# Attention and two feed-forward layers on one core: a plain second slot, and later low parts of W_out

## The chip, the cores and the metric

The kernel runs on one core of one Trainium2 chip. The metric is the device time of one execution in microseconds (us). The kernel before takes 766.02 us (median of 3 runs, 765.67 to 766.97).

## The reference

Attention over 2 batches, 8 heads, 768 positions and 64 elements a head, in which a query sees only the keys whose nearest of 16 centroids is its own, then two feed-forward layers on 1536 tokens (512 to 2048 to 512 elements):

```python
mask = q_assign[:, :, :, None] == k_assign[:, :, None, :]
scores = np.where(mask, scale * np.matmul(q, k.transpose(0, 1, 3, 2)), -1e9)
attn = np.exp(scores - np.max(scores, axis=-1, keepdims=True))
x = np.matmul(attn / (np.sum(attn, axis=-1, keepdims=True) + 1e-09), v)
...
h = x @ w_in;  x = (h * (1.0 / (1.0 + np.exp(-1.702 * h)))) @ w_out
h = x @ w_in2; r = np.maximum(h, 0.0); out = (r * r) @ w_out2
```

The four weight matrices come as 64-bit floats. The kernel reads their bits and makes 32-bit floats of them on the chip.

## The kernel before, in words

**Precision.** TensorE multiplies with operands of the type fp32r. A matrix is split in a high part (ACT's cast) and a low part (what is left, by DVE), and a product of two matrices is three products: high by high, high by low, low by high.

**Order.** The attention takes up the first third. The feed-forward layers follow in 32 slots, `q` = 0 to 31: two layers, two batches of 768 tokens, and `NP` = 8 slots of 256 hidden elements each. The first pass is slots 0 to 7, layer 0 for batch 0. Every engine works through its own queue in the order in which the program issues the instructions; this order is written out by hand in the loop over `slots` (from L1084 on), and the tile framework puts in the waits. SP's queue holds nearly all DMAs.

**A slot** makes two chunks of 128 hidden elements (`ga` and `gb`) for 768 tokens, in four blocks of 128 by 384 in two banks of PSUM, A and B_. The plain form (`hidden`, L143) needs four block products of 12 matmuls each. The other form (`product`, L1006) is Strassen's scheme in Winograd's order: seven products of 6 matmuls, from sums of blocks of x (S1 to S4, `folds`, L160) and of W_in (T1 to T4, `Weights.sums`, L976). For it ACT copies three products from PSUM to SBUF and DVE adds three others to them (`total`, L860; DVE's rows with L864). `active` (L868) is the gelu, twice on ACT (L876 the high part, L877 in full), and `low` (L879) the low part on DVE (L880). Slot 0 is plain, slots 1 to 31 are Strassen's.

**The parts of W_in.** `Weights` holds the two chunks of a slot in `wb` and their block sums in `wt`. `sums` is four DVE operations (L979 to L982). `early(0)`, `early(1)` and `late` split them in high and low parts (`part`: ACT L985, DVE L986). The first two products need `early(0)`, the next two `early(1)`, the last three `late`.

**W_out's work.** `second` (L882) multiplies the gelu's result by W_out; a slot leaves it to the next one, which does it in four quarters of 12 matmuls, `before(0)` to `before(3)`, between its own products. In slots 2 to 7 the first two quarters take chunk `gb`, the other two `ga`.

**Decoding.** Every 128 rows or columns of a weight matrix are one task (`tasks`, L1020), in an order fixed ahead: W_in and W_out of the first pass by turns. A task goes through these steps: `fetch` (L1027), a DMA of 512 KB on SP into one of three raw buffers; `absolute` (L1033), the magnitude on ACT (L98 and L100); `step(0)` and `step(1)`, the decoding on DVE (L112 and L115); and `step(2)`, which writes a W_in task to DRAM (`keep`, L136; its DMA is L138) or splits a W_out task (`parts`, L119: ACT's cast L121, DVE's low part L122), and asks for the fetch of the task three further on. `COUNTS` (L1013) says how many tasks a slot does: 2 in slot 0, 4 each in slots 1 to 6, 1 in slot 7. All W_out tasks of the first pass use one tile, `room`, so the magnitude of one waits until the one before it has been split. W_in tasks go into `wb`.

**The order in slots 1 to 7** (from L1138 on): A gets the product B11 with A11, ACT copies it to `h`; B_ gets B21 with A12; first task; `total(0, LO)`; quarter 0; second task; products T2 and T1 (A and B_ again, after ACT's copy and after the total); sums and `early` of the next slot; quarter 1; products T3 and B22; the third task with its split; `total(1, HI)` and `total(1, LO)`; the gelu of `gb`; the fourth task; quarter 2; product T4, which needs A back from `total(1, HI)`; quarter 3. In slots 3 to 6 there is one more DVE operation (`nxt.sum`, L946), in slot 7 five splittings of batch 1's x (`nxt.part`).

**The way from the attention to slot 1.** In the last 14 tiles of the attention GpSimd splits the four quarters of batch 0's x (L792, L793) and folds them to S1 to S4 (L796), beside the merges of the heads' results (L588) and the normalisation (L616). Behind the loop DVE decodes chunk 2 of W_in (`mags[4]`), SP fetches the raw data of chunk 3 into the buffer that this sets free and then the norms' rows (`spread`), and DVE does the last merge. Chunk 2 is copied by a DMA into `weights[1]` (L1072) and split (`early(0)`, L1073). In slot 0 chunk 3 is decoded; then come the sums and `early(1)` for slot 1, the magnitude and decoding of chunk 4, and the splitting of S1 to S4 (`fold`, L955) between them.

## Time and profile before

| | |
|---|---|
| time, median of 3 runs | 766.02 us (765.67 to 766.97) |
| the profiled execution's own time | 766.92 us |
| its span, first to last instruction | 765.1 us |
| granted TensorE clock, mean over the span | 0.995 |
| busy: PE, DVE, ACT, GpSimd | 97%, 76%, 74%, 22% |
| the first pass of the feed-forward layers | about 244 to 378 us |

In the rows, times are us from the first instruction; L12 is line 12 of the kernel. PE is TensorE's matmuls (PEld its weight loads, which overlap them), DVE is VectorE, ACT ScalarE, POOL GpSimd and SP the queue that issues DMAs. In a timeline a row gives the start, the time it took, the engine, the line, what it writes and reads with its shape, and how many like it were merged to one row. In square brackets stand the idle time of the engine before it and what ended that. One instruction overlaps the next of its engine a little, so that the distance between two starts is shorter than the time of the first. A granted clock of 1.00 is 2.4 GHz, one of 0.50 is 1.2 GHz.

### The profile page before, as it was taken

How to read it: one execution, taken by the hardware profiler on the slowest of the kernel's cores; microseconds unless marked ns; L12 is line 12 of the kernel's file. 1: busy time of each engine (PE TensorE's matmuls, PEld its weight loads, DVE VectorE, ACT ScalarE, POOL GpSimd, SP SyncE). 2: the span in 40 equal slices, each digit the busy share in tenths (PEclk: the TensorE clock that was granted, in tenths of full speed). 3: DMA queues.
4: the chain of work that ended last, by engine and by line, in shares of the span. 5: the costliest groups of instructions: out<-in, count | busy, mean ns of one | idle time of the engine just before them, and what ended most of it. 6: DMA issues, size and time to landing. Idle time of an engine off the chain costs nothing.

```text
span 765.1 us, 12063 instructions
## 1 busy us (share of the span) xinstructions
PE 744.8 (97%) x4303; PEld 680.0 (89%) x4303; DVE 579.0 (76%) x1011; ACT 568.0 (74%) x1138; POOL 169.3 (22%) x226
## 2 busy tenths in 40 slices
PE   8999999999999599999999999999999999999998
PEld 5999999999999588888899999998899898988996
DVE  7988998988997888888776777777776787553441
ACT  7999999999898777787686666767767676553441
POOL 5848667667675000000000000000000000000000
PEclk9999999999999899999999999999999999999999
DMA  8886676794222545445154233313443203101002
GB/s 211 176 205 141 137 195 196 157 210 98 68 52 59 173 164 174 156 160 180 56 169 162 99 122 110 119 61 97 153 149 111 83 29 112 54 28 56 0 1 83
DMA packets 72235, 91.15 MB, mean 119 GB/s; under 512 B 30384, under 2 KB 54096, under 8 KB 72080
## 3 DMA queue, kind: packets, MB, share of 16 engines
q1 hardware_dynamic: 71632, 90.26, 41.1%
q8 instruction: 34, 0.56, 0.3%
q14 instruction: 25, 0.20, 0.1%
q10 hardware_dynamic: 544, 0.13, 0.1%
HBM read 61.12 MB, written 13.94 MB: 98 GB/s over the span
## 4 chain that ended last, share of the span: by engine, by line
PE 79%; DVE 10%; ACT 8%; issue 1%; DMA 0%; POOL 0%; DVEq 0%; ACTq 0%; SPq 0%; POOLq 0%
PE ps L1010 23%; PE y L899 17%; PE pa L565 8%; PE pt L540 8%; PE y L893 6%; PE ps L516 4%; PE ps L518 4%; PE y L895 3%; ACT gh L876 2%; ACT h L877 2%; PE ps L369 1%; DVE h L864 1%; DVE rr L112 1%; ACT oh L121 1%; PE pt L306 1%
## 5 line engine op out<-in xcount | busy, mean ns | idle before, releaser
L553 DVE TENSOR_TENSOR el<-pt,eh 128x384 fp32r<-128x384 f32 x192 | 97.6, 550 | 11.1 <-ACT eh L550 10.4
L522 DVE TENSOR_REDUCE nm<-ps 128x1 f32<-128x768 f32 x96 | 91.5, 954 | 11.6 <-PE ps L518 10.0
L876 ACT ACTIVATE gh<-h 128x384 fp32r<-128x384 f32 (+1 forms) x72 | 47.8, 664 | 60.6 <-DVE h L866 32.3
L531 ACT ACTIVATE e<-ps,nm 128x768 f32<-128x768 f32 x96 | 87.7, 913 | 2.8 <-DVE nm L522 2.3
L550 ACT CAST eh<-pt 128x384 fp32r<-128x384 f32 x192 | 83.2, 489 | 5.7 <-PE pt L540 4.0
L880 DVE TENSOR_TENSOR gl<-h,gh 128x384 fp32r<-128x384 f32 (+1 forms) x97 | 65.7, 681 | 22.2 <-ACT h L877 14.3
L540 PE MATMUL pt<-identF,e 128*128 128x128 f32 x576 | 80.2, 274 | 0.8 <-DVE el L553 0.6
L899 PE MATMUL y<-oh,gl 128*128 128x512 f32 x192 | 75.2, 391 | 0.0
L899 PE MATMUL y<-ol,gh 128*128 128x512 f32 x192 | 75.0, 390 | 0.0
L899 PE MATMUL y<-oh,gh 128*128 128x512 f32 x192 | 74.9, 390 | 0.0
L1010 PE MATMUL ps<-xh,wxh 128*128 128x384 f32 x248 | 64.9, 343 | 8.6 <-ACT h L1144 7.8
L516 PE MATMUL ps<-k,q 128*128 128x512 f32 x192 | 68.9, 361 | 1.0 <-ACT e L531 1.0
L540 PEld LDWEIGHTS pt<-identF,e 128*128 128x128 f32 x576 | 65.3, 140 | 3.2 <-DVE el L553 2.4
L1010 PE MATMUL ps<-xl,wxh 128*128 128x384 f32 x248 | 64.2, 340 | 0.0
L1010 PE MATMUL ps<-xh,wxl 128*128 128x384 f32 x248 | 63.9, 339 | 0.0
L518 PE MATMUL ps<-k,q 80*128 80x512 f32 x192 | 60.9, 340 | 0.0
L1010 PEld LDWEIGHTS ps<-xh,wxh 128*128 128x128 f32 x248 | 43.3, 190 | 12.9 <-ACT h L1144 8.1
L1010 PE MATMUL ps<-xh,wyh 128*128 128x384 f32 x186 | 48.0, 339 | 4.9 <-DVE h L864 4.9
L893 PE MATMUL y<-gl,oh 128*128 128x512 f32 x128 | 50.2, 392 | 0.0
L893 PE MATMUL y<-gh,ol 128*128 128x512 f32 x128 | 50.1, 392 | 0.0
L893 PE MATMUL y<-gh,oh 128*128 128x512 f32 x128 | 50.1, 392 | 0.0
L877 ACT ACTIVATE h<-h 128x384 f32<-128x384 f32 (+1 forms) x72 | 47.8, 665 | 2.3
(223 smaller groups left out, 1884.5 us busy)
## 6 DMA issues: line engine op xcount, KB each, us to landing
raw<-in_moe_w_in_dram SPq DMA_DIRECT2D x32, 512.0 KB, 4.1
raw<-in_moe_w_out_dram SPq DMA_DIRECT2D x32, 512.0 KB, 4.2
wb<-wst SPq DMA_DIRECT2D x24, 512.0 KB, 4.3
q<-k SPq DMA_DIRECT2D x15, 384.0 KB, 5.8
wst<-room SPq DMA_DIRECT2D x16, 256.0 KB, 2.4
wst<-wb SPq DMA_DIRECT2D x13, 256.0 KB, 2.5
k<-k SPq DMA_DIRECT2D x16, 192.0 KB, 5.1
rawv<-in_v_dram SPq DMA_DIRECT2D x8, 384.0 KB, 4.9
```

What stands on the lines that cost most here:

```text
L516: nc.tensor.matmul(ps[:, a:a + n], q2[:, qs], k2[:, a:a + n], start=True, stop=False)
L518: nc.tensor.matmul(ps[:, a:a + n], q1[0:K1, qs], k1[0:K1, a:a + n], start=False, stop=True)
L522: nc.vector.tensor_reduce(out=nm, in_=live["s", t][:, 0:S], op=ALU.max, axis=AX, negate=True)
L531: nc.scalar.activation(e, live["s", t][:, 0:S], ACTF.Exp, bias=live.pop(("nm", t)), accum_out=sums[:, s:s + 1])
L540: nc.tensor.transpose(pt[:, i], e[:, kc * P:(kc + 1) * P], identF)
L550: nc.scalar.copy(place("eh", t, u), live["pt", t, u])
L553: nc.vector.tensor_tensor(out=place("el", t, u), in0=live.pop(("pt", t, u)), in1=f32(place("eh", t, u)), op=ALU.subtract)
L876: nc.scalar.activation(g[0][:, at], src, of)
L880: nc.vector.tensor_sub(g[1][:, at], h[:, c, at], f32(g[0][:, at]))
L893: nc.tensor.matmul(y[m], l[:, cs], r[:, 0:512], start=first, stop=last)
L899: nc.tensor.matmul(y[m], l[:, m * P:(m + 1) * P], r, start=(begin and z == 0), stop=(fc == KF - 1 and z == 2))
L1010: nc.tensor.matmul(ps, w[a][:, wi, kc * P:(kc + 1) * P], x[z][kc], start=start and j == kc == 0, stop=j == 2 and kc == 1, skip_group_check ...
```

## The change

- **Slot 1 becomes plain.** It takes a branch of its own: four times `hidden`, with the parts of the two W_in chunks as they are (`Weights.plain` splits them into the tile that held B11, B21, T1 and T2, `sides` are its two halves), the gelu straight from PSUM, no sums, no late parts, no copies and no totals. The DMA that copied chunk 2 into `weights[1]` is gone. The order of its tasks and quarters is written anew: quarters 0 and 1 behind the second block product, 2 and 3 behind the fourth.
- **The splitting of S1 to S4** moves from slot 0 to slot 1. Slot 0 keeps the plain split of chunk 3, the decoding of chunk 4 and now the magnitude of the next task too.
- **Slots 2 to 7:** the low part of a split W_out task (DVE, L122) is held back. For the first one it comes behind the decoding of the second task; for the third one behind the two totals and the first decoding step of the fourth task (in slot 6 behind the totals, ahead of the fourth task's magnitude). The fourth magnitude comes ahead of the third task's split (in slot 6 behind the gelu of `gb`).
- **GpSimd in the attention's last tiles:** its operations for x begin one tile earlier and stand in every other tile; the fourth fold comes behind the loop, after the last merges.
- **The order of W_out's chunks** in slot 1 is `ga` first, as in slot 0.

```diff
--- before.py
+++ after.py
@@ -786,13 +786,13 @@
             if blk > 1 and part == 2:
                 merged(blk - 2)
 
-            if end in (1, 3, 5, 7):
+            if end in (0, 2, 4, 6):
                 at = quarters[end // 2]
                 hi, lo = xs[at] = quarter(t3_p, "t3")
                 nc.gpsimd.tensor_copy(hi, a[at])
                 nc.gpsimd.tensor_tensor(out=lo, in0=a[at], in1=f32(hi), op=ALU.subtract)
-            elif 9 <= end < 13:
-                dst, x, y, op = folds(a)[end - 9]
+            elif end in (8, 10, 12):
+                dst, x, y, op = folds(a)[end // 2 - 4]
                 nc.gpsimd.tensor_tensor(out=dst, in0=x, in1=y, op=op)
 
             for i, at in enumerate((t + LEAD - GT, t + LEAD - 2 * GT, t + LEAD - 3 * GT, t + LEAD - 4 * GT)):
@@ -829,6 +829,8 @@
             av(blk, part)
         merge(blk, True)
         merged(blk, nc.vector)
+        dst, x, y, op = folds(a)[3]
+        nc.gpsimd.tensor_tensor(out=dst, in0=x, in1=y, op=op)
         first.append(hidden(xs, w1, 1))
         spread(NG - 1)
         return w1, raw, xs, mags, first, lambda: norm(NG - 1)
@@ -989,10 +991,16 @@
             self.x = (wx_p.tile([P, 4, 2 * P], F32R, tag="wx", name="wxh"),
                       wp_b[1].tile([P, 4, 2 * P], F32R, tag="wx", name="wxl"))
 
-        def early(self, i, src=None):
+        def plain(self, c, src):
+            if not c:
+                self.x_tiles()
+            self.part(*self.x, slice(2 * c, 2 * c + 2), src)
+            self.sides = [[x[:, 2 * i:2 * i + 2, :].rearrange("p a n -> p (a n)") for x in self.x] for i in range(2)]
+
+        def early(self, i):
             if i == 0:
                 self.x_tiles()
-                self.part(*self.x, slice(0, 2), self.wb[:, 2:4, :] if src is None else src)
+                self.part(*self.x, slice(0, 2), self.wb[:, 2:4, :])
             else:
                 self.part(*self.x, slice(2, 4), wt[:, 0:2, :])
 
@@ -1069,8 +1077,7 @@
     second_w = [wy_p.tile([P, 3 * 2 * P], F32R, tag=n, name=n)[:, 0:DM] for n in ("wyh", "wyl")]
     parts(f32(mags[2][1]), *second_w, nc.vector)
     keep(0, 2, f32(mags[4][1]))
-    nc.sync.dma_start(weights[1].chunk(2), f32(mags[4][1]))
-    weights[1].early(0, f32(mags[4][1]).rearrange("p (a n) -> p a n", a=2))
+    weights[1].plain(0, f32(mags[4][1]).rearrange("p (a n) -> p a n", a=2))
     wo[0, 1] = out_tiles(1)
     parts(f32(words(mags[3][0])[0]), *wo[0, 1], nc.vector)
     fetch()
@@ -1101,6 +1108,10 @@
             if p == 0 and ends:
                 finish(*ends, k)
 
+        def release():
+            while held:
+                held.pop(0)()
+
         def do(i, ks):
             if i < n:
                 for k in ks:
@@ -1124,17 +1135,46 @@
                 if not c:
                     for k in range(3):
                         step(k)
-            wn.sums()
-            wn.early(1)
+            wn.plain(1, wn.wb[:, 0:2, :])
+            absolute()
+            for k in range(3):
+                step(k)
+            absolute()
+        elif q == 1:
+            weights[q + 2] = Weights(slots[q + 2][0], slots[q + 2][2], False)
+            bank[0] = hidden(xs, wq.sides[0], 0, A)
+            active(layer, ga, 0, LO, A)
+            absolute()
+            do(0, (0, 1))
+            low(ga, 0, LO)
+            bank[1] = hidden(xs, wq.sides[0], 1, B_)
+            active(layer, ga, 0, HI, B_)
+            do(0, (2,))
+            do(1, (0, 1, 2))
+            low(ga, 0, HI)
+            before(0)
+            before(1)
+            ph = hidden(xs, wq.sides[1], 0)
+            active(layer, gb, 1, LO, ph)
             absolute()
             combos.fold(Combos.S2)
-            step(0)
-            step(1)
+            do(2, (0, 1))
+            low(gb, 1, LO)
+            ph = hidden(xs, wq.sides[1], 1)
+            wn.sums()
+            active(layer, gb, 1, HI, ph)
+            wn.early(0)
+            wn.early(1)
             combos.fold(Combos.S1)
-            step(2)
+            low(gb, 1, HI)
             absolute()
+            do(2, (2,))
+            before(2)
+            before(3)
+            do(3, (0, 1, 2))
             combos.fold(Combos.S3)
             combos.fold(Combos.S4)
+            absolute()
         elif q < NP:
             at_bank = 1 - at_bank
             x = combos.tiles
@@ -1150,10 +1190,12 @@
             total(layer, 0, LO, B_)
             active(layer, ga, 0, LO)
             do(0, (1,))
+            held = []
             do(0, (2,))
             before(0)
+            do(1, (0, 1, 2))
+            release()
             low(ga, 0, LO)
-            do(1, (0, 1, 2))
             product(A, wq.x, wq.T2, x[Combos.S2])
             nc.scalar.copy(h[:, 1, LO], A)
             if last:
@@ -1170,12 +1212,21 @@
             wn.early(1)
             product(A, wq.y, wq.T3, x[Combos.S3])
             product(B_, wq.y, wq.B22, x[Combos.S4])
+            absolute()
             do(2, (2,))
-            absolute()
             total(layer, 1, HI, A)
             total(layer, 1, LO, B_)
             active(layer, gb, 1, ALL)
-            do(3, (0, 1, 2))
+            if q == NP - 2:
+                release()
+                absolute()
+                do(3, (0,))
+            else:
+                do(3, (0,))
+                release()
+            do(3, (1, 2))
+            release()
+            held = None
             if last:
                 nxt.part(3)
             before(2)
@@ -1364,7 +1415,7 @@
         if p == 0 and q:
             y = y_tiles()
         pend = second(layer, y, [(g, 2 * p + i) for i, g in enumerate((ga, gb))],
-                      None if p == NP - 1 else (1, 0) if q else (0, 1))
+                      None if p == NP - 1 else (1, 0) if q > 1 else (0, 1))
         ends = (layer, y, b)
     for k in range(4):
         pend[k]()
```

## Rows read from the trace of the kernel before

**Rows 1.** The page's first part: TensorE's busy time and share.

```profile
PE 744.8 (97%) x4303; PEld 680.0 (89%) x4303; DVE 579.0 (76%) x1011; ACT 568.0 (74%) x1138; POOL 169.3 (22%) x226
```

**Rows 2.** The waits on PE: us in total, times, longest.

```profile
PE ps L1010 <- DVE h L864: 5.6, 8, 1.4
```

**Rows 3.** A window of one slot's length: PE, PEld, DVE, ACT, POOL busy, clock, DMA.

```profile
310.93:327.53 16.60, 15.93 (x91) 14.65 (x90) 14.64 (x27) 13.11 (x24) 0.00 (x0) 1.00 0.48 159
```

**Rows 4.** PE's timeline: start us, us, line, tiles, count, [idle before <-releaser].

```profile
262.76 1.01 PE L1010 MATMUL ps<-xh,wxh 128*128 128x384 f32 x2 [7.80 <-ACT h L1144]
...
291.22 0.62 PE L1010 MATMUL ps<-xh,wyh 128*128 128x384 f32 x2 [0.69 <-DVE h L864]
...
294.46 0.52 PE L1010 MATMUL ps<-xh,wxh 128*128 128x384 f32 x2
...
302.84 0.51 PE L1010 MATMUL ps<-xh,wyh 128*128 128x384 f32 x2
...
304.57 0.51 PE L1010 MATMUL ps<-xh,wyl 128*128 128x384 f32 x2
...
307.82 0.62 PE L1010 MATMUL ps<-xh,wyh 128*128 128x384 f32 x2 [0.66 <-DVE h L864]
...
357.62 0.61 PE L1010 MATMUL ps<-xh,wyh 128*128 128x384 f32 x2 [0.66 <-DVE h L864]
...
366.98 0.61 PE L1010 MATMUL ps<-xh,wxh 128*128 128x384 f32 x2 [0.71 <-DVE h L864]
```

**Rows 5.** Windows around the stall's end: columns as in rows 3.

```profile
259.00:260.00 1.00, 0.00 (x0) 0.00 (x0) 0.96 (x2) 0.97 (x3) 0.00 (x0) 0.86 0.00 0
...
266.50:267.00 0.50, 0.50 (x4) 0.50 (x3) 0.40 (x1) 0.45 (x2) 0.00 (x0) 0.95 0.37 63
```

**Rows 6.** DVE's timeline in slots 1 and 3.

```profile
260.26 2.68 DVE L122 TENSOR_TENSOR xl<-x,xh 128x768 fp32r<-128x768 f32 x3
...
299.77 0.69 DVE L122 TENSOR_TENSOR ol<-rr,oh 128x512 fp32r<-128x512 f32 x1 [0.98 <-ACT oh L121]
...
300.38 0.55 DVE L880 TENSOR_TENSOR gl<-h,gh 128x384 fp32r<-128x384 f32 x1
...
302.37 0.42 DVE L979 TENSOR_TENSOR wt<-wb 128x256 f32<-128x256 f32 x1
...
304.44 0.69 DVE L112 SCALAR_TENSOR_TENSOR rr<-raw,rr 128x512 uint32<-128x512 uint32 x1
...
305.82 0.67 DVE L986 TENSOR_TENSOR wxl<-wt,wxh 128x512 fp32r<-128x512 f32 x1
...
306.61 0.69 DVE L122 TENSOR_TENSOR ol<-rr,oh 128x512 fp32r<-128x512 f32 x1
...
307.21 1.02 DVE L864 TENSOR_TENSOR h<-ps,h 128x384 f32<-128x384 f32 x2
```

**Rows 7.** ACT's timeline in slots 1 and 2.

```profile
257.19 1.55 ACT L121 CAST xh<-x 128x768 fp32r<-128x768 f32 x2
...
291.67 0.85 ACT L876 ACTIVATE gh<-h 128x768 fp32r<-128x768 f32 x1 [0.37 <-DVE h L864]
...
293.30 0.48 ACT L876 ACTIVATE gh<-ps 128x384 fp32r<-128x384 f32 x1
...
294.04 0.68 ACT L98 ACTIVATE rr<-raw 128x512 bf16<-128x512 bf16 x1
...
295.38 0.60 ACT L985 CAST wyh<-wt 128x512 fp32r<-128x512 f32 x1
```

**Rows 8.** GpSimd beside DVE: the timeline of all engines.

```profile
242.66 0.68 DVE L112 SCALAR_TENSOR_TENSOR raw<-raw,raw 128x512 uint32<-128x512 uint32 x1
...
250.44 1.84 POOL L616 TENSOR_TENSOR x<-x,rr 128x768 f32<-128x768 f32 x1 [8.10 <-DMA rr<-row]
...
250.61 2.22 DVE L112 SCALAR_TENSOR_TENSOR wb<-raw,wb 128x512 uint32<-128x512 uint32 x1 [0.75 <-ACT wb L100]
```

**Rows 9.** The page's DMA issues: line, count, KB, median us to landing.

```profile
raw<-in_moe_w_in_dram SPq DMA_DIRECT2D x32, 512.0 KB, 4.1
```

## The prediction

> **What bounds the kernel now.** I read the engines' shares first, then who waits on PE, then the timelines around each wait. PE is busy 97% of the span [rows 1], so only its pauses can give much. Nearly all lie in the first pass (slots 0 to 7). There is one stall of 7.80 us, up to 262.76, for ACT's copy of the first product out of PSUM [rows 4]: that copy stands in ACT's queue behind the four folds and two magnitudes. PE went idle at 254.96, had the full clock until about 259.7 (the window 259 to 260 averages 0.86), and has it back at about 266.55 (0.95 over the half us behind 266.50) [rows 5]. The stretch 262.76 to 266.55 ran at 1.2 instead of 2.4 GHz, which cost half of its 3.8 us, 1.9. The other pauses are 8 waits on DVE's additions out of PSUM, 5.6 us together [rows 2]: each slot stands before T4 until DVE has done `total(1, HI)`.
>
> **The length of a slot.** T4 starts at 291.22 in slot 2 and at 307.82 in slot 3, 16.60 apart [rows 4]. PE's own work is less: from 302.84 to 304.57 ten matmuls start, 0.173 each, so a product of six takes 1.04, and the last two, from 304.57 on, end at 304.92; from T4 at 291.22, less 1.04 and 0.1 for its slow first pair, to 294.46 a quarter of the W_out work takes 2.1. T4 could have begun at 304.92 + 2.1 = 307.0, not 307.82. So an unbroken slot takes 16.60 - 0.8 - 0.1 = 15.7. DVE is the engine that sets the 16.60: in a slot of that length it is busy 14.64 [rows 3], and it stands still 0.98 before one low part of W_out, which waits for ACT's cast [rows 6].
>
> **The change: leaving the attention.** GpSimd's four splittings start one tile earlier each; their first reader, PE's first W_in matmul, comes only at the end of the attention, so I cost that at nothing; without this cover it would be the 1.84 of a GpSimd operation on 768 elements. The fourth fold moves behind the last merge, to about 242.4, where DVE decodes chunk 2 (242.66, 0.68 us [rows 8]). A fold is such an operation too. Against one (GpSimd 250.44 to 252.28) the same DVE instruction took 2.22, 1.54 more [rows 8]. So the decode loses 0 to 1.54; I take 1.5, since it has the same shape and meets GpSimd already at work. Behind it on SP stand the fetch for chunk 3 and the DMA of the norms' rows, both later by as much. What hides most of it: chunk 3's decode itself stood behind GpSimd's norm. I put its end at 254.2 instead of 250.61 + 2.22 + 0.7 = 253.5.
>
> By the rule of the Trainium skill, SBUF — State Buffer, section "SBUF: two separate sides", the shared port is an exclusive lock for the whole instruction, and whichever of a GpSimd operation and a DVE operation with two SBUF inputs starts first keeps it. The trace agrees on the loser (2.22 against 0.68); by the rule the sum would be this one, and nothing below needs it. It speaks against this move of the fold.
>
> **Slots 0 and 1.** The stall began behind two products and a quarter, 4.2 us, so slot 1 begins at about 250.6. The plain slot has 48 matmuls for 42, 6 x 0.173 = 1.0 more. In return DVE loses four block sums and three low parts, ACT the late casts and three copies, and the SBUF copy of chunk 2 leaves SP. PE has four times 2.1 of W_in and four times 2.1 of W_out work: 250.6 + 16.8 = 267.4, if nothing stops it. The third of the W_in parts needs the first bank back: ACT does a cast of 0.6, two magnitudes of 1.34 (294.04 to 295.38) and a gelu pair of 0.74 (293.30 to 294.04) [rows 7] from 254.2 on, 258.2; PE comes there at 259.0. So the 7.8 and the 1.9 go.
>
> What is late next is DVE. Chain: chunk 3's decode ends 254.2, its raw buffer is refetched, 0.5 of issue and 4.1 to landing [rows 9], 258.8. On ACT, which takes its queue in order, then come a magnitude, a gelu pair, W_out's cast (0.5), a gelu pair, a magnitude and the cast of S2 (1.55 for two [rows 7]): 1.34 + 0.74 + 0.5 + 0.74 + 1.34 + 0.8 = 5.5, 264.3. From there DVE has no pause, and I price it by the distances between starts [rows 6]: a fold 0.9 (2.68 for three), a decode 1.4 (304.44 to 305.82), a low part 0.5, W_out's low part 0.6, the block sums with the first weight part 2.07 (302.37 to 304.44), the second weight part 0.6, the late parts 0.95, a total 0.5. In order, slot 1: S2 0.9, decode 1.4, low 0.5, sums 2.07 (this ends at 269.2), second part 0.6, S1 0.9, low 0.5, W_out 0.6, decode 1.4, S3 and S4 1.8; slot 2: late 0.95, half a decode 0.7, total 0.5, half 0.7, decode 1.4, W_out 0.6, low 0.5, sums 2.07, decode 1.4, second part 0.6. Together 20.1: 284.4, and the total(1, HI) behind it ends at 284.95. T4 of slot 2 begins at 285.0 instead of 291.22: **-6.2**. PE pauses on the way: 267.4 to 269.3 for the weight part, about 2 for the copy out of the first bank, 0.8 before T1, 0.5 before T4; some 5 in all instead of 7.8 + 1.9 + the waits of two slots.
>
> **Slots 3 to 6.** W_out's two low parts leave the place in front of the totals: 0.98 of idle, 0.6 of work (306.61 to 307.21) and 0.1 between, 1.7 in all, and T4 needs 0.8. DVE's 14.64 then fit into PE's 15.7. What moves: W_out's low part comes 1.3 later than now, behind the next decoding; its first reader, the next slot's first W_out quarter, stands 1.1 + 2.1 + 2.1 = 5.3 behind T4, which covers it; without that cover PE would pay the 1.3. The magnitude, 1.34, goes ahead of W_out's cast and the gelus on ACT; the cast waits for DVE's decoding there anyway. Each slot gives 0.9 (0.66 by the idle alone): four slots **-3.7**.
>
> **Slots 6 and 7.** In slot 6 the last decoding shares one buffer with the W_out chunk before it, so its magnitude now stands behind the gelus. PE ends the second product before T4 by 2.1, DVE its two totals 1.5 before T4. From there on ACT and DVE: gelus 1.63 (291.67 to 293.30), magnitude 1.34, decode 1.4, cast 0.6, gelu pair 0.74: T4 + 4.2, just when PE wants that bank. DVE goes on from T4 + 3.45 with W_out 0.6, low 0.9, sum 0.9, low 0.5, then waits for ACT's magnitude, late casts and a cast of x until T4 + 7.5, then 0.9 + 0.7 + 0.55: T4 + 9.65 for T1, which PE alone would reach at T4 + 8.5. Now it is 366.98 - 357.62 = 9.36 [rows 4]. I take **+0.5** (bounds 0 and 1.5).
>
> **Sum.** -6.2 - 3.7 + 0.5 = -9.4. Behind slot 7 PE has no pause now, so all of it should reach the end. The profiled execution has a span of 765.1 and took 766.92; the median is 766.02. Forecast: span 755.7, median **756.6**.
>
> **Rivals.**
> 1. The wait moves on: DVE and ACT need 16.6 a slot in any order, for instance because the cast is late again behind the magnitude. For it: DVE is busy 14.64 and ACT 13.11 [rows 3], each waiting on the other. Against it: 1.7 is taken out of the stretch. Only the 6.2 less 0.5 remain: 760.3. Chance 0.13.
> 2. Pauses near 2 us already lower the clock. For it: several come within 18 us. Against it: the stall ran 4.8 us before the clock fell [rows 5]. One fall costs 1.9: 758.5. Chance 0.12.
> 3. DVE keeps ahead and half or more of the 5 us of pauses in slots 1 and 2 do not come, or slot 7 loses nothing: 753.9. Chance 0.12.
> 4. Slower: magnitudes stand earlier on ACT and meet their fetch. A raw chunk is asked for three decodings before; the fourth magnitude of each of slots 2 to 6 now wants it about when it lands, 4.1 after the issue [rows 9]. ACT is in order, so gelus and bank releases wait behind it. Some 2.2 are free (0.4 on ACT, 1.8 before PE's W_out quarter); then every us is lost five times. The gain of 9.4 is gone from 9.4 / 5 + 2.2 = 4.1 more on, a landing of 8.2; at 8.6 it gives 768. Only a landing twice as long does this. Chance 0.03.
> 5. It does not do what it says: slot 1's third W_in part stands for ACT as long as PE stands now (the copies of ACT only change their names), and the totals keep their wait: 766. Chance 0.04.
>
> The forecast itself has 0.56, within 755.0 and 758.0. The range 753.8 to 760.6 takes in cases 1 to 3 and the bounds above. Some 0.2%, 1.5 us, is what a measurement of this kernel can tell from no change; faster by more 0.93, within 0.04, slower 0.03.
>
> **What would show it.** Right: no wait of PE above 2.5 us behind the attention and the full clock throughout slots 0 to 2; T4 at 285 in slot 2; T4 to T4 near 15.7 in slots 3 to 6, without the wait for DVE; one of about 1 us for T1 in slot 7; DVE's decode at 242.7 at about 2.2. Wrong: a granted clock of 0.50 in slots 1 or 2; a T4 distance that stays at 16.6; ACT standing for a fetch; PE waiting for W_out's low parts.

## The result, and the profile after

The changed kernel takes **759.37 us** (median of 4 runs, 758.85 to 760.14), the kernel before 766.50 in the runs beside it (4 runs, 765.67 to 767.08). The ratio is 0.9909 (95% interval 0.9891 to 0.9926): faster by 7.1 us, where 9.4 were forecast. The profiled execution took 759.83 us with a span of 758.0, against 765.1.

The first part of the page of the kernel after, beside [rows 1]:

```profile
PE 744.2 (98%) x4309; PEld 680.4 (90%) x4309; DVE 574.9 (76%) x1003; ACT 565.0 (75%) x1135; POOL 169.7 (22%) x226
```

PE's busy time fell by 0.6 us while the span fell by 7.1: what went is idle time of PE. Which idle time, the waits on PE of the kernel after show (us in total, times, longest; beside [rows 2]):

```profile
PE ps L1018 <- ACT h L1184: 2.2, 1, 2.2
PE ps L1018 <- DVE h L866: 1.7, 3, 1.0
PE ps L1018 <- DVE wxl L988: 1.5, 1, 1.5
...
PE ps L1018 <- ACT h L879: 1.0, 1, 1.0
```

In this kernel L1018 is a product (L1010 before), L866 a total (L864), L988 a low part of W_in (L986), L879 the second gelu (L877), L1184 the copy of a product out of PSUM (L1144). The 7.80 us stall is gone, and of the 8 waits for a total 3 are left. In their place stand some shorter pauses, none above 2.2. (Line numbers differ by a few from kernel to kernel; operation and tiles name a row.) PE's timeline of the kernel after says where (beside [rows 4]):

```profile
261.09 0.96 PE L150 MATMUL ph<-xh,wxh 128*128 128x384 f32 x4 [0.42 <-ACT h L879]
...
269.81 0.62 PE L1018 MATMUL ps<-xh,wxl 128*128 128x384 f32 x2 [1.51 <-DVE wxl L988]
...
275.75 0.61 PE L1018 MATMUL ps<-xh,wxh 128*128 128x384 f32 x2 [2.20 <-ACT h L1184]
...
277.57 0.67 PE L1018 MATMUL ps<-xh,wxh 128*128 128x384 f32 x2 [0.50 <-DVE h L866]
...
286.52 0.52 PE L1018 MATMUL ps<-xh,wyh 128*128 128x384 f32 x2
...
349.06 0.52 PE L1018 MATMUL ps<-xh,wyh 128*128 128x384 f32 x2
...
354.41 0.62 PE L1018 MATMUL ps<-xh,wxh 128*128 128x384 f32 x2 [1.00 <-ACT h L879]
...
359.82 0.61 PE L1018 MATMUL ps<-xh,wxh 128*128 128x384 f32 x2 [0.98 <-DVE h L866]
...
367.56 0.61 PE L1018 MATMUL ps<-xh,wyh 128*128 128x384 f32 x2 [0.18 <-DVE h L866]
```

The rows at 286.52, 349.06 and 367.56 are T4 in slots 2, 6 and 7. In slots 2 to 6 it starts without any wait, and from slot 2 to slot 6 the steps are (349.06 - 286.52) / 4 = 15.63 each.

Absolute times of two executions can't be compared to a tenth. The code up to the decoding of chunk 2 is the same on DVE, and yet that decoding started anywhere from 241.66 to 243.45 in the profiled executions of this study (242.66 before, 241.95 after). So I take the start of that decoding as the **origin** and compare distances from it:

| from | to | before | after | gained | forecast |
|---|---|---|---|---|---|
| origin | T4 of slot 2 | 48.56 | 44.57 | 4.0 | 6.2 |
| T4 of slot 2 | T4 of slot 6 | 4 x 16.60 | 4 x 15.63 | 3.9 | 3.7 |
| T4 of slot 6 | T4 of slot 7 | 17.10 | 18.50 | -1.4 | -0.5 |

Together 6.5; the profiled execution began 0.7 earlier too, which makes the span's 7.1. So two terms need an explanation: 2.2 us of the first, 0.9 of the last. The timelines of DVE and GpSimd in the kernel after hold 0.8 of the first (beside [rows 8]):

```profile
241.71 1.83 POOL L833 TENSOR_TENSOR x<-x 128x768 f32<-128x768 f32 x1
241.95 2.15 DVE L112 SCALAR_TENSOR_TENSOR raw<-raw,raw 128x512 uint32<-128x512 uint32 x1
...
251.17 0.69 DVE L112 SCALAR_TENSOR_TENSOR wb<-raw,wb 128x512 uint32<-128x512 uint32 x1 [2.02 <-ACT wb L100]
251.18 2.39 POOL L616 TENSOR_TENSOR x<-x,rr 128x768 f32<-128x768 f32 x1 [7.63 <-DMA rr<-row]
251.90 2.29 DVE L115 SCALAR_TENSOR_TENSOR wb<-raw,wb 128x512 uint16<-128x512 uint16 x1
...
284.54 1.00 DVE L866 TENSOR_TENSOR h<-ps,h 128x384 f32<-128x384 f32 x2
...
345.37 0.69 DVE L112 SCALAR_TENSOR_TENSOR rr<-raw,rr 128x512 uint32<-128x512 uint32 x1 [0.63 <-ACT rr L100]
...
347.33 1.02 DVE L866 TENSOR_TENSOR h<-ps,h 128x384 f32<-128x384 f32 x2
```

The fourth fold (L833) made the decoding of chunk 2 take 2.15. Then the norm (L616) met the decoding of chunk 3 all the same, at its second step. That decoding ended at 254.19, 12.24 behind the origin; before it was 10.95. The totals of slot 2 start at 284.54, 42.59 behind the origin. PE can start 0.6 behind the start of such a pair (before: 307.21 and 307.82 [rows 4, 6]), at 285.15. It started at 286.52. The windows of the kernel after (columns as in [rows 3]) show what held it:

```profile
277.50:278.00 0.50, 0.43 (x2) 0.43 (x3) 0.50 (x2) 0.45 (x1) 0.00 (x0) 0.99 0.07 25
278.00:279.00 1.00, 1.00 (x6) 1.00 (x4) 0.97 (x3) 0.97 (x3) 0.00 (x0) 0.50 0.04 16
...
280.00:281.00 1.00, 1.00 (x4) 0.83 (x4) 0.97 (x4) 1.00 (x3) 0.00 (x0) 0.50 0.97 309
281.00:282.00 1.00, 1.00 (x6) 0.89 (x5) 1.00 (x4) 0.97 (x3) 0.00 (x0) 0.80 1.01 347
```

From about 278.0 to 281.4 the granted clock is 1.2 GHz, although no pause before it was longer than 2.20 us: 3.4 us at half speed lose 1.7, of which 1.4 (from 285.15 to 286.52) reached T4.

### The profile page after: what moved, and what is told of

It is laid out like the page before. It is cut to its first block, busy times and chain, and to the rows that moved or that the text cites. A ratio compares the mean times of both kernels' runs of the same rounds, so it can differ in the third digit from the quotient of the medians.

```text
span 758.0 us, 12069 instructions
## 1 busy us (share of the span) xinstructions
PE 744.2 (98%) x4309; PEld 680.4 (90%) x4309; DVE 574.9 (76%) x1003; ACT 565.0 (75%) x1135; POOL 169.7 (22%) x226
## 4 chain that ended last, share of the span: by engine, by line
PE 87%; DVE 6%; ACT 4%; DMA 1%; issue 1%; POOL 0%; SPq 0%; ACTq 0%; POOLq 0%
PE ps L1018 27%; PE y L901 17%; PE y L895 9%; PE pt L540 8%; PE pa L565 8%; PE y L897 5%; PE ps L516 4%; PE ps L518 4%; PE ps L369 1%; PE pt L306 1%; DVE nm L522 1%; DVE xl L122 1%; PE pm L395 1%; DMA raw<-in_moe_w_in_dram 1%; DVE el L553 1%
## 5 line engine op out<-in xcount | busy, mean ns | idle before, releaser
L1018 PE MATMUL ps<-xh,wxh 128*128 128x384 f32 x240 | 62.2, 340 | 4.8 <-ACT h L1184 2.2
L1018 PE MATMUL ps<-xh,wxl 128*128 128x384 f32 x240 | 61.8, 339 | 1.5 <-DVE wxl L988 1.5
L1018 PE MATMUL ps<-xl,wxh 128*128 128x384 f32 x240 | 61.7, 339 | 0.0
L1018 PEld LDWEIGHTS ps<-xh,wxh 128*128 128x128 f32 x240 | 41.4, 188 | 9.2 <-ACT h L1184 2.5
L988 DVE TENSOR_TENSOR wxl<-wb,wxh 128x512 fp32r<-128x512 f32 x31 | 21.4, 691 | 37.2 <-ACT wxh L987 28.5
L868 DVE CUSTOM_DVE_ANT_0 h<-ps,h 128x384 f32<-128x384 f32 x48 | 25.7, 553 | 29.6 <-PE ps L1018 29.0
```

The costliest lines, as they stand in the source:

```text
L1018: nc.tensor.matmul(ps, w[a][:, wi, kc * P:(kc + 1) * P], x[z][kc], start=start and j == kc == 0, stop=j == 2 and kc == 1, skip_group_check ...
```

## The experiments

All times are medians; "behind the origin" has the meaning above. A time is compared with the kernel before in the same runs, by the ratio.

### The two halves of the change

The first kernel is the kernel before with the new order of slots 2 to 7 alone (slot 1 stays Strassen's); the second is the changed kernel with the order of slots 2 to 7 put back.

```diff
--- kernel before
+++ holding_back_alone
-            do(0, (2,))
-            before(0)
-            low(ga, 0, LO)
-            do(1, (0, 1, 2))
+            if q == 1:
...
+            else:
+                held = []
+                do(0, (2,))
+                before(0)
+                do(1, (0, 1, 2))
+                release()
+                low(ga, 0, LO)
...
```

```diff
--- kernel after
+++ no_holding_back
-            held = []
             do(0, (2,))
             before(0)
-            do(1, (0, 1, 2))
-            release()
             low(ga, 0, LO)
+            do(1, (0, 1, 2))
...
-            absolute()
             do(2, (2,))
+            absolute()
...
+            do(3, (0, 1, 2))
```

> Edit: the kernel before with the second half of the change alone: in slots 2 to 7 the low parts of W_out are held back and the fourth magnitude moves; slot 1 stays Strassen's, with the stall of 7.8. Theory (the order gives 0.97 a slot by itself and costs 1.4 in slot 7): T4 to T4 is 15.64 in slots 3 to 6 and 18.5 in slot 7; slot 2 gains up to 0.95; time about 3.4 under the kernel before, 763.2. Rival (the order helps only once the plain slot has let DVE get ahead): T4 to T4 stays near 16.6, 766.5.

> Edit: the changed kernel without the second half of the change: slots 2 to 7 in the old order, no low part held back. Theory (the order alone gives 0.97 a slot): T4 to T4 is 16.6 again in slots 3 to 6, with a wait of 0.7 for DVE each, 3.9 in all; slot 7 takes 17.1 instead of 18.5 again; 759.4 + 3.9 - 1.4 = 761.9. Rival (the first wait only moved and the plain slot brought all): 759.4.

Measured: **763.68 us** (762.62 to 765.45), ratio 0.9969 (0.9957 to 0.9981) for the order alone, and **763.80** (762.59 to 764.29), ratio 0.9956 (0.9944 to 0.9969) for the change without it. PE's timeline of the order alone:

```profile
261.78 1.01 PE L1010 MATMUL ps<-xh,wxh 128*128 128x384 f32 x2 [7.57 <-ACT h L1148]
...
289.42 0.52 PE L1010 MATMUL ps<-xh,wyh 128*128 128x384 f32 x2
...
305.05 0.52 PE L1010 MATMUL ps<-xh,wyh 128*128 128x384 f32 x2
```

and of the change without the order:

```profile
270.69 0.62 PE L1018 MATMUL ps<-xh,wxl 128*128 128x384 f32 x2 [1.53 <-DVE wxl L988]
...
276.63 0.62 PE L1018 MATMUL ps<-xh,wxh 128*128 128x384 f32 x2 [2.20 <-ACT h L1184]
...
288.10 0.63 PE L1018 MATMUL ps<-xh,wyh 128*128 128x384 f32 x2 [2.07 <-DVE h L866]
...
337.86 0.62 PE L1018 MATMUL ps<-xh,wyh 128*128 128x384 f32 x2 [0.66 <-DVE h L866]
...
354.45 0.63 PE L1018 MATMUL ps<-xh,wyh 128*128 128x384 f32 x2 [0.66 <-DVE h L866]
```

The order alone brings steps of 15.63 from slot 2 on (289.42 to 305.05), with the stall of 7.57 untouched; without the order, slots keep 354.45 - 337.86 = 16.59 and the wait of 0.66 for the total. So the order of slots 2 to 7 is what made a slot 16.60 long, as the prediction had it. The two moves in it, W_out's low parts on DVE and the fourth magnitude on ACT, were made together; no run shows them apart.

The two halves act in different places. By distances in the profiled executions the plain slot alone gains 3.0 up to T4 of slot 2 (48.56 to 45.54 behind the origin), the order alone 3.5 (1.0 in slot 2, 4 x 0.97 up to slot 6, less 1.4 in slot 7), and both together 6.5. By the ratio the order alone gains less, 2.4 us (1.5 to 3.3); why, no run shows.

The second kernel was 1.9 us slower than expected. The expectation had left out slot 2, which has the new order as well: without it T4 there waits 2.07 for the total. Counted by distances the order is worth 0.97 in slot 2 (45.54 behind the origin against 44.57), which accounts for half of the 1.9, and 4 x 0.96 in the next four, less the 1.4 that it costs in slot 7: 3.4 us. By the ratios, 0.9956 against 0.9909, it is 3.6. The 0.97 is what the clock left over: the totals of slot 2 come 2.3 sooner with the order (42.59 behind the origin against 44.93), but the clock fell in that execution of the changed kernel and not in this one.

### GpSimd's fold and the decodings

The first kernel puts GpSimd's operations back to the tiles where they were. The second does that too, and moves the norm that meets chunk 3's decoding from GpSimd to DVE, behind that decoding.

```diff
--- kernel after
+++ old_gpsimd_order
-            if end in (0, 2, 4, 6):
+            if end in (1, 3, 5, 7):
...
-            elif end in (8, 10, 12):
-                dst, x, y, op = folds(a)[end // 2 - 4]
+            elif 9 <= end < 13:
+                dst, x, y, op = folds(a)[end - 9]
...
-        dst, x, y, op = folds(a)[3]
-        nc.gpsimd.tensor_tensor(out=dst, in0=x, in1=y, op=op)
```

```diff
--- old_gpsimd_order
+++ norm_on_dve
-        def norm(gi):
+        def norm(gi, engine=nc.gpsimd):
...
-            nc.gpsimd.tensor_tensor(out=dst, in0=dst, in1=live["rr", gi], op=ALU.mult)
+            engine.tensor_tensor(out=dst, in0=dst, in1=live["rr", gi], op=ALU.mult)
...
-        return w1, raw, xs, mags, first, lambda: norm(NG - 1)
+        return w1, raw, xs, mags, first, lambda: norm(NG - 1, nc.vector)
...
-    last_norm()
-    room = rpool.tile([P, S], F32, tag="rr", name="rr")[:, 0:DM]
...
             wn.plain(1, wn.wb[:, 0:2, :])
+            last_norm()
+            room = rpool.tile([P, S], F32, tag="rr", name="rr")[:, 0:DM]
```

> Edit: the changed kernel with GpSimd's splittings and folds where the kernel before has them, the fourth fold inside the loop. Theory (the fold's collision with the decode of chunk 2 costs 1.5 there, of which all but 0.5 is hidden behind the norm): that decode takes 0.68 instead of 2.15, chunk 3's decode ends about 0.5 sooner, T4 of slot 2 comes up to 0.5 sooner; time 758.9 to 759.4. Rival (nothing hides it): the whole 1.5, 757.9.

> Edit: the changed kernel with the old order of GpSimd's folds and the last normalisation on DVE, behind the plain split of slot 0, instead of GpSimd. Theory (the collisions of GpSimd's last two operations with DVE's decodes pass through to T4 of slot 2, since everything behind chunk 3's decode is one chain): no DVE decode near the attention's end takes more than 0.8; chunk 3's decode ends about 9.5 us behind the start of chunk 2's instead of 12.2, T4 of slot 2 comes 2.0 to 3.5 sooner than in the changed kernel, of which half the clock can take back; time 756 to 757.5. Rival (the old order of the folds already gave all there is): as the kernel with the old GpSimd order, 758.6.

Measured: **758.58 us** (757.32 to 760.48), ratio 0.9894 (0.9879 to 0.991), and **758.32** (757.99 to 758.51), ratio 0.9894 (0.9881 to 0.9907). DVE's and GpSimd's timelines with the old order on GpSimd:

```profile
242.23 0.68 DVE L112 SCALAR_TENSOR_TENSOR raw<-raw,raw 128x512 uint32<-128x512 uint32 x1
...
249.72 1.84 POOL L616 TENSOR_TENSOR x<-x,rr 128x768 f32<-128x768 f32 x1 [7.81 <-DMA rr<-row]
250.19 1.92 DVE L112 SCALAR_TENSOR_TENSOR wb<-raw,wb 128x512 uint32<-128x512 uint32 x1 [0.77 <-ACT wb L100]
252.14 0.75 DVE L115 SCALAR_TENSOR_TENSOR wb<-raw,wb 128x512 uint16<-128x512 uint16 x1
...
283.44 1.02 DVE L864 TENSOR_TENSOR h<-ps,h 128x384 f32<-128x384 f32 x2
```

Without the fold there, chunk 2's decoding takes 0.68 again. Chunk 3's ends at 252.89, 10.66 behind the origin instead of 12.24, and the totals of slot 2 start 41.21 behind it instead of 42.59: the fold's 1.5 us come through almost whole, 1.4, where at most 0.5 was expected. (In five profiled executions of kernels with the same orders on DVE, ACT and GpSimd up to these totals, the totals stand 42.04 to 42.76 behind the origin, so it is 0.8 to 1.6.) What was to hide most of the 1.5 hides nothing, because the norm is delayed by the same 1.5: its row of DMA stands on SP behind the fetch that waits for chunk 2. It starts 7.49 behind the origin here and 9.23 in the changed kernel, and meets chunk 3's decoding in both.

The norm itself costs nothing further, against the theory, which had 756 to 757.5; the rival's 758.6 is what came. With it on DVE, chunk 3's decoding ends 9.45 behind the origin, 1.2 earlier still, and the totals stand at 283.61, the same 41.21. ACT's timeline of that kernel says where the 1.2 went:

```profile
255.68 0.66 ACT L98 ACTIVATE rr<-raw 128x512 bf16<-128x512 bf16 x1 [1.37 <-DMA raw<-in_moe_w_out_dram]
...
261.03 0.49 ACT L876 ACTIVATE gh<-ph 128x384 fp32r<-128x384 f32 x1 [0.60 <-PE ph L150]
```

ACT now stands 1.37 for the raw data of W_out and 0.60 for PE's third block, and the chain behind it begins no earlier. In both medians the gain of 1.4 is about the size of what the intervals leave open; it is shown by the traces, not by the times.

### The clock in slot 2

This kernel adds 13 matmuls of zeros in the pause before T2 of slot 2; they add zero to the sums of W_out's work. It ran twice, the second time (filled_again) beside the changed kernel itself (changed_again), in the same runs.

```diff
--- kernel after
+++ filled_pause
+    idle = m_p.tile([P, 352], BF16, name="idle")
+    nc.vector.memset(idle, 0.0)
...
             low(ga, 0, LO)
+            for _ in range(13 if q == 2 else 0):
+                nc.tensor.matmul(y[0][:, 0:352], idle[:, 0:P], idle, start=False, stop=False, skip_group_check=True)
             product(A, wq.x, wq.T2, x[Combos.S2])
```

> Edit: the changed kernel with 13 matmuls by zeros (352 columns, about 0.15 us each, 1.9 in all) added into the W_out sums in slot 2's pause before T2; they add nothing to the result. Theory (the half clock behind that pause, 278.0 to 281.6, costs 1.4 to 1.8, since DVE's total(1, HI) is done at 285.05 and T4 starts only at 286.52): the granted clock stays at 1.00 through slot 2, T4 starts at about 285.1, 1.4 sooner; time 758.0 where the run without them has the fall. Rival (the clock falls in some executions only and the median hardly feels it, or DVE would hold T4 anyway): 759.4.

> Edit: the kernel with the 13 zero matmuls in slot 2's pause once more. Theory (the fall costs 1.4 to 1.9 where it happens): T4 of slot 2 at 42.7 behind the start of chunk 2's decode, the median 0.7 to 1.9 under the changed kernel of the same job. Rival (executions differ more by their start than by the clock): no difference between the two medians.

> Edit: none, the changed kernel once more, beside the next one on the same chip. Theory (half clock behind slot 2's pause in most executions, at 1.4 to 1.9 each): the mean granted clock is under 1.000 in most executions, the median about 759.4. Rival (it falls in half of them): as many at 1.000.

Measured: **759.22 us** (758.92 to 760.29), ratio 0.9905 (0.989 to 0.992); again **759.17** (758.27 to 759.85), ratio 0.99 (0.9885 to 0.9915); the changed kernel beside it **759.99** (758.84 to 760.48), ratio 0.9907 (0.9891 to 0.9924). PE's timeline, DVE's totals and one of the windows of the first:

```profile
276.04 0.61 PE L1020 MATMUL ps<-xh,wxh 128*128 128x384 f32 x2 [0.24 <-ACT h L1186]
...
284.82 1.03 DVE L868 TENSOR_TENSOR h<-ps,h 128x384 f32<-128x384 f32 x2
...
285.44 0.61 PE L1020 MATMUL ps<-xh,wyh 128*128 128x384 f32 x2
```

```profile
278.00:279.00 1.00, 1.00 (x6) 1.00 (x7) 1.00 (x2) 0.97 (x3) 0.00 (x0) 1.00 0.06 25
```

With the pause filled, the clock stays at 1.00 through slot 2 in both profiled executions, and T4 stands right behind the totals, 0.62 and 0.60 behind their start. In the two of the changed kernel, which both fell to 0.50, it stands 1.98 and 2.01 behind it. So where the fall comes in this kernel it costs T4 1.4 us. Behind the origin T4 stands 42.66 and 43.36 against 44.57 and 44.51; there the spread of the totals comes in.

The medians do not resolve it: 759.17 and 759.99 with overlapping intervals, so the rival of filled_again stands as far as times go. Of the 8 executions of the changed kernel, 5 have a mean granted clock of 0.998 and 3 of 1.000, so the fall may not come in all. But the mean does not say where the clock fell, two of the 8 with the pause filled have 0.997 and 0.998 too, and the three at 1.000 (760.14, 758.90, 758.84) are not faster than the rest (758.85 to 760.48).

The other profiled executions with a plain slot 1 say more. PE paused 2.03 to 2.21 before T2 of slot 2 in seven of them: in the two of the changed kernel, in no_holding_back, and in old_gpsimd_order, norm_on_dve, slot6_old_order and slot1_order. In six of these the clock fell to 0.50, and T4 stood 1.30 to 2.01 behind the start of the totals. In the four with 0.24 to 0.93 there (the two with the pause filled, and the last two kernels below) it stayed at 1.00, with 0.59 to 0.62. A short pause there kept the clock each time; a long one mostly lost it.

What decides it in the long ones is **left open**. The seventh, the change without the new order, paused 1.53, 2.20 and 0.52 before the same instructions as the changed kernel and kept the full clock; its windows (columns as in [rows 3]):

```profile
278.00:280.00 2.00, 1.53 (x9) 1.49 (x10) 1.08 (x2) 1.52 (x4) 0.00 (x0) 1.00 0.31 125
280.00:282.00 2.00, 2.00 (x14) 1.79 (x13) 1.89 (x4) 1.97 (x6) 0.00 (x0) 1.00 0.74 220
```

The Trainium skill, TensorE: Matmul & The Clock Gate, section "Part 1: The HAM clock gate (the "warmup" mystery)", says that the chip judges TensorE's activity by a count of its own that does not start with the kernel, so that the moment of a change varies between executions. Equal pauses with and without a fall agree with that; no run here shows it directly.

### Slot 6

The changed kernel, with slot 6's third and fourth task in the order of the kernel before.

```diff
--- kernel after
+++ slot6_old_order
+            if q == NP - 2:
+                do(2, (2,))
+                release()
+                held = None
             absolute()
-            do(2, (2,))
+            if q != NP - 2:
+                do(2, (2,))
...
-            if q == NP - 2:
-                release()
-                absolute()
-                do(3, (0,))
-            else:
-                do(3, (0,))
-                release()
+            do(3, (0,))
+            release()
```

> Edit: the changed kernel, but slot 6 splits its third task ahead of the totals and does the fourth magnitude ahead of the gelus, as the kernel before does. Theory (slot 7's pauses of 1.0 for the bank and 1.0 for T1 come from the fourth magnitude standing behind the gelus in slot 6): the total(1, HI) of slot 6 comes 0.7 later, which T4 at 349.06 does not feel; the decode starts 1.9 sooner; slot 7 has no wait for ACT's gelu and at most 0.5 for T1; T4 to T4 from slot 6 to slot 7 falls from 18.5 to about 16.7, the time by 1.8, to 757.6. Rival (the order in slot 6 does not matter, DVE is late in slot 7 in any order): 759.4.

Measured: **758.29 us** (757.09 to 759.65), ratio 0.9889 (0.9875 to 0.9902). PE's timeline:

```profile
348.99 0.52 PE L1018 MATMUL ps<-xh,wyh 128*128 128x384 f32 x2
...
365.79 0.63 PE L1018 MATMUL ps<-xh,wyh 128*128 128x384 f32 x2 [0.18 <-DVE h L866]
```

The step from T4 to T4 is 16.80, against 18.50: 1.7 us of the changed kernel are lost by slot 6's own order. The wait of 1.00 for the bank is gone, and that for T1 is 0.54 instead of 0.98. So the wait at 354.41 in the kernel after comes from that order: on ACT's timeline there the fourth magnitude, and the cast that waits for its decoding, stand ahead of the gelu that sets PE's bank free.

```profile
350.01 0.65 ACT L98 ACTIVATE rr<-raw 128x512 bf16<-128x512 bf16 x1
...
352.96 0.62 ACT L121 CAST oh<-rr 128x512 fp32r<-128x512 f32 x1 [1.54 <-DVE rr L115]
353.49 0.48 ACT L878 ACTIVATE gh<-ps 128x384 fp32r<-128x384 f32 x1
```

### The order in slot 1, and all of it together

The chain that sets slot 2 runs through ACT and DVE. This kernel takes work of others out of its way in slot 1: the second block's gelu ahead of a magnitude, W_out's low part held back, the block sums ahead of the folds.

```diff
--- kernel after
+++ slot1_order
             bank[0] = hidden(xs, wq.sides[0], 0, A)
+            bank[1] = hidden(xs, wq.sides[0], 1, B_)
             active(layer, ga, 0, LO, A)
+            active(layer, ga, 0, HI, B_)
             absolute()
...
-            bank[1] = hidden(xs, wq.sides[0], 1, B_)
-            active(layer, ga, 0, HI, B_)
+            low(ga, 0, HI)
+            held = []
             do(0, (2,))
             do(1, (0, 1, 2))
-            low(ga, 0, HI)
+            release()
...
+            wn.sums()
             absolute()
-            combos.fold(Combos.S2)
...
-            wn.sums()
...
             wn.early(1)
+            combos.fold(Combos.S2)
             combos.fold(Combos.S1)
```

> Edit: the changed kernel with another order in slot 1: both gelus of ga ahead of the third magnitude, W_out's low part held back behind the next decode, the block sums and early parts ahead of the folds S2 and S1. Theory (T4 of slot 2 is set by one chain: DVE has 2.05 of idle before W_out's low part and 0.77 before S2, and no pause behind that): DVE's work behind it comes about 2.2 sooner, slot 2's first weight part is there in time (no wait of PE for it), total(1, HI) of slot 2 starts 40.4 us behind DVE's decode of chunk 2 instead of 42.6; time 756 to 757.5. Rival (ACT's queue or the clock sets T4 of slot 2): T4 and the time stay, 759.4.

Measured: **757.96 us** (757.06 to 758.8), ratio 0.989 (0.9877 to 0.9902). The totals of slot 2 start at 283.52, 40.07 behind the origin of 243.45, 2.5 earlier than in the changed kernel, and T4 42.04 behind it. So the order of ACT's and DVE's queues in slot 1 sets when T4 of slot 2 can begin. Nothing behind it takes the gain back: from T4 of slot 2 to the end of the span there are 471.5 us in both kernels. The clock fell there too (0.55 from 278 to 280).

Then the edits together: all_four_edits has slot 6's and GpSimd's old orders, the norm on DVE and the new order of slot 1; three_edits has the same without the norm on DVE.

> Edit: the changed kernel with four edits: slot 6 in the old order, GpSimd's folds in the old order, the last normalisation on DVE, and the new order of slot 1. Theory (the three losses are separate links of one chain, and add until PE alone sets the pace): T4 of slot 2 about 39 us behind the start of chunk 2's decode instead of 44.6, slot 6 to slot 7 16.8 instead of 18.5; time about 752 to 753.5. Rival (PE or ACT becomes the bound after the first of them): 755 or more.

> Edit: as the kernel with all four edits, but the last normalisation stays on GpSimd. Theory (once the fold is out of the way, PE's third block and the fetches set the pace of slot 1, so that the normalisation's collision is hidden): as with all four, 754.2; T4 of slot 2 39.5 behind the start of chunk 2's decode. Rival (with the new order of slot 1 the collision's 1.2 passes through): T4 at 40.7, 755.4.

Measured: **754.22 us** (753.59 to 755.83), ratio 0.9844 (0.9832 to 0.9857), and **753.54** (752.9 to 754.1), ratio 0.9827 (0.9812 to 0.9842). The second is the best version: 6.45 us below the changed kernel in the same runs (759.99). PE is busy 99% of its span. PE's timeline:

```profile
271.62 0.62 PE L1016 MATMUL ps<-xh,wxh 128*128 128x384 f32 x2 [0.93 <-ACT h L1185]
...
281.20 0.62 PE L1016 MATMUL ps<-xh,wyh 128*128 128x384 f32 x2
...
343.87 0.52 PE L1016 MATMUL ps<-xh,wyh 128*128 128x384 f32 x2
...
360.65 0.61 PE L1016 MATMUL ps<-xh,wyh 128*128 128x384 f32 x2 [0.18 <-DVE h L864]
```

T4 of slot 2 stands 281.20 - 241.66 = 39.54 behind the origin, 5.0 less than in the changed kernel (44.51 in the same runs), and from T4 of slot 6 to T4 of slot 7 it takes 16.78 instead of 18.50, 1.7 less: together 6.7, about the whole difference of the medians. The pause for the copy out of the first bank is 0.93 instead of 2.20, and in this execution the clock did not fall in slot 2. Moving the norm to DVE on top of that brings nothing: with all four edits T4 of slot 2 stands 39.53 behind the origin.

## Why the prediction was right, and what it missed

The direction, its two places and the range held; the forecast was 2.8 us too good.

- **The stall and its clock.** Right: 7.80 and what it cost at half clock are gone, because slot 1 has no copy and no total (the plain slot without the new order has no such stall, the order with Strassen's slot 1 keeps 7.57). PE's longest wait behind the attention is 2.20, where I had bound it by 2.5.
- **The chain of slots 1 and 2.** Right in its length: from the end of chunk 3's decoding to the totals I had 284.4 - 254.2 = 30.2 us, and the trace has 284.54 - 254.19 = 30.35. It is the chain: slot1_order shortened it and T4 followed. That it fits to 0.2 is partly luck. ACT began it at 258.85, where I had 258.8, but then took 6.0 us to the fold of S2 and not 5.5, mainly because a magnitude stood 0.39 for the raw data of W_out, which I had not looked at; DVE, without a pause from there as foreseen, took 19.7 and not 20.1.

```profile
262.70 0.67 ACT L98 ACTIVATE rr<-raw 128x512 bf16<-128x512 bf16 x1 [0.39 <-DMA raw<-in_moe_w_out_dram]
...
264.88 0.96 DVE L122 TENSOR_TENSOR xl<-x,xh 128x768 fp32r<-128x768 f32 x1 [0.77 <-ACT xh L121]
```

- **The pauses.** I had 1.9 for the weight part (counted from a slot 1 that begins at 250.6; 254.96 - 4.2 gives 250.8), 2 for the bank, 0.8 for T1 and 0.5 for T4, and none at slot 1's third block; they were 1.51, 2.20, 0.50 and two times none. The fourth block, which I had not looked at, waited 0.42 for the second bank (the row at 261.09); it had no consequence, as the chain on DVE ended last.
- **"What hides most of it: chunk 3's decode itself stood behind GpSimd's norm"** is the step that failed in the first term. The price, 1.5, was right (2.15 against 0.68). I took 0.7 of it as coming through; at the end of chunk 3's decoding 1.3 came in this execution (12.24 against 10.95), and at the totals 1.4 by the experiment. The prediction itself named why: the norms' rows stand on SP behind the same fetch. So the norm is delayed with the decoding that it collides with. In the kernel after, DVE's first step began 0.01 ahead of the norm, ran at its own 0.69 and made GpSimd take 2.39 instead of 1.84; then the second step, 0.75 when alone, paid with 2.29. In changed_again, the same kernel, the norm began 0.04 ahead, took its own 1.84, and DVE's first step paid:

```profile
251.64 1.84 POOL L616 TENSOR_TENSOR x<-x,rr 128x768 f32<-128x768 f32 x1 [7.59 <-DMA rr<-row]
...
251.68 2.35 DVE L112 SCALAR_TENSOR_TENSOR wb<-raw,wb 128x512 uint32<-128x512 uint32 x1 [2.02 <-ACT wb L100]
```

The rule that the prediction cites from the Trainium skill, SBUF — State Buffer, section "SBUF: two separate sides", that the one which starts first keeps the shared port for its whole instruction, fits both. Either way chunk 3's decoding ended late, 12.24 and 12.36 behind the origin.
- **The clock** was my second rival, at 0.12: "pauses near 2 us already lower the clock". It came on top of the forecast in the profiled execution and cost 1.4 of T4's time there, where I had priced a fall at 1.9. So the full clock that I had put down as a sign of being right did not hold, and the granted clock of 0.50 in slot 2, a sign of being wrong, came. I had argued against it from one stall that ran 4.8 us before the clock fell [rows 5]. That row shows that the clock can last so long, not that it must.
- **Slots 3 to 6.** Right: 15.63 where I had 15.7, and no wait for DVE at T4. No wait took the removed one's place (first rival), no magnitude met its fetch there (it did in slots 0 and 1), and all of DVE's work went into PE's slot.
- **Slots 6 and 7** were mis-sized: +1.4 where I took +0.5, within the bounds 0 and 1.5. The step that failed is "DVE its two totals 1.5 before T4". They ended at 347.33 + 1.02 = 348.35, 0.7 before it. DVE had stood 0.63 at 345.37 for ACT's third magnitude. All that I counted from there on ACT came 0.8 later: the bank, which I had free just when PE wants it, came 1.00 too late, and T1 waited the 0.98 that I had foreseen.

The sum with the measured sizes: forecast span 755.7; + 0.8 (0.6 of the collision, 0.2 elsewhere in the chain) + 1.4 (clock) + 0.9 (slot 7) - 0.2 (slots 3 to 6) - 0.7 (the earlier start) = 757.9, where the profile has 758.0.

## What to carry to other kernels

When a step is moved past others on a queue, ask what else is delayed with it: a cover that hangs on the same queue moves along and hides nothing. In a chain over two engines that work in order, a lead of a microsecond is soon used up by one operation that stands ahead of the one that matters; put what frees a buffer or a bank of PSUM ahead of what only prepares later work. And where PE pauses several times in a row, look at the granted clock before counting the pauses as plain idle time.

## What the runs showed that I had not expected

- TensorE's granted clock fell to 0.50 behind three separate pauses of 1.51, 2.20 and 0.50 us, with PE at work between them, while in another kernel nearly the same three left it at 1.00. In slot1_order it fell behind two of 2.03 and 0.66, in old_gpsimd_order behind two of 0.93 and 2.21.
- Between executions the start of the same instruction, 242 us into the program, moved by 1.8 us (241.66 to 243.45); in the kernel after, a lead over the kernel before was there as early as PE's first scores (12.15 against 13.24). A gain of 1 us was to be read only by distances from a common instruction.
- A GpSimd operation that loses against DVE is made longer too: 2.39 for 1.84.
